# Attention, MoE and a second MLP on one core: scales from sums on ScalarE, the mask inside the minus product, steps laid out anew

## Chip, core and metric

The kernel runs on one core of a Trainium2 chip. The metric is the time of one execution on the device in microseconds. TensorE is called PE here, VectorE DVE, ScalarE ACT, GpSimd POOL and SyncE SP, as in the profile.

## What is computed

Three stages, all in float32 at the interface:

```python
# chunked attention: B=4, H=8, S=768, D=64, chunks of 32, 16 keys left and 8 right, 8 memory keys
scores = scale * q_c @ k_full.T            # k_full = 8 memory keys, then the chunk's window
a = exp(scores - scores.max(-1)); a /= a.sum(-1) + 1e-9
out[:, :, c] = a @ v_full
# MoE: N=3072 tokens, D=512, E=8 experts, F=1024
P = exp(x @ w_gate - max)
for _ in range(8): P /= P.sum(1) + 1e-9; P /= P.sum(0) + 1e-9; P *= N / E
x = sum over e of P[:, e] * (relu(x @ w1[e]) @ w2[e])
# second MLP: 512 to 2048 to 512
out = relu(x @ w_in) ** 2 @ w_out
```

## The kernel before

**Numbers.** Every float32 operand of a matmul is split into a high and a low float16 part, and a product is three float16 matmuls (low by high, high by low, high by high). Before the split an operand is multiplied by a power of two, which a maximum of absolute values sets.

**Attention tiles.** There are 32 tiles of 96 queries. A tile goes through the steps of the table `STEPS`: `load` (five to seven DMAs, issued on SP for the first three tiles and on ACT after that), `mx` (L260: DVE's maximum of absolute values of q, k and v by row, then exponent and cast to `ae`), `row` (L270: PE turns the row values into three rows), `row_mx` (L277, L278: DVE reduces them to three values and puts these on a diagonal `ad`), `all` (L283: PE spreads them to all partitions), `scale` (DVE), `hi` (L326: ACT's high parts), `lo` (L332: DVE's low parts; they free the raw buffer), `tqk` (L338: a transposing DMA on SP), `scores` (L356 adds the mask by a product with a one-hot matrix, L368 the products of q and k), `max` (DVE: maximum over keys, split into `m`), `mt` (L387: PE transposes the maxima), `mtc` (L395: ACT copies them), `st` (L403: the transposed mask; L414: the transposed scores; L417: minus the maxima, by a product with the matrix `minus`), `exp` (L426), `ahi`, `alo` (the split of the exponentials on ACT and POOL), `av` (L447 to L455: the product with v), `norm`, `xhi`, `xlo` (L464 to L481) and `tx` (L491: a transposing DMA into the token tile `xt`). The scores stand in three PSUM buffers, which `scores` and `st` share.

Raw q, k and v of a tile stand in one of three buffers, from tile 18 on in one of two.

**The order.** It is written out by hand. Each step of tile i is put into a list at a planned time, and the list is sorted by it; each engine then runs its own instructions in that order:

```python
def ta(i):
    return T0 + sum(TS[:i]) + TA * max(0, i - len(TS))

def when(i, n):
    r = min(1.0, i / RAMP)
    t = ta(i) + (1 - r) * STEPS[n][1] + r * STEPS[n][0]
    if n == "load" and i >= 3:
        prev = max(m for m in range(i) if raw_of(m) == raw_of(i))
        t = max(t, when(prev, "lo") + LDO)
    return t
```

So from tile 6 on the first offset of a step counts alone, and tiles follow each other by `TA`. Between the steps of the attention tiles stand the units of the first expert: four pairs (`l1_pair`, 24 matmuls of 256 columns) and four halves (`l2_half`, 12 matmuls of 512 columns) for every 256 tokens, each unit 2.65 x `STR` planned units after the one before it, and not before `done(i)`, which is `tx` plus 4, of the last tile they need, plus `DN[1]`. `gate` (eight small matmuls, and a copy by ACT at L515) stands at the start of each block, moved by `DN[2]`.

**After attention.** The gate's weights are balanced in eight rounds on DVE, PE and ACT, beside the end of the first expert. Experts 1 to 7 and the second MLP follow, the later ones with Strassen-like products of seven blocks, whose small steps are put off by the numbers of items in `LAG` and `W1B`. L1133 there makes the low parts of such operands.

**Set-up.** `setup_const` fills the constants, most of them on POOL.

Of the kernel before, what the change touches and what calls it, by code (L numbers as in the profile page):

```python
# [7 lines left out]
F32 = mybir.dt.float32  # L8
# [16 lines left out]
    "all": (2.56, 1.20),  # L25
    "scale": (4.56, 1.59),
    "hi": (7.00, 2.19),
    "lo": (8.20, 2.60),
    "tqk": (15.08, 6.30),
    "scores": (26.35, 11.37),  # L30
    "max": (27.25, 12.18),
    "mt": (30.80, 13.20),
    "mtc": (31.00, 13.30),
    "st": (33.80, 14.20),
    "exp": (34.80, 15.20),
    "ahi": (36.80, 16.20),
    "alo": (37.00, 16.30),
    "av": (42.00, 19.20),
    "norm": (42.60, 19.90),
    "xhi": (45.20, 21.70),  # L40
    "xlo": (47.14, 21.80),
    "tx": (53.00, 23.20),
}
L1LAG = 1.730
T0 = 5.969
TS = [6.83, 3.31, 5.80, 8.23, 10.00]
TA = 10.957
# [4 lines left out]
W_AT = [-5.06, 6.92, 9.11, 14.42, 18.96, 23.87, 33.67, 39.86, -3.33, 28.00, 3.81]  # L52
# [3 lines left out]
DN = [-0.34, 0.00, 0.08]  # L56
# [10 lines left out]
W1B = [[1, 2, 2, 5], [2, 3, 6, 8]]  # L67

LAG = [{"11": [2, 3], "22": [14, 15], "12": [3, 4], "relu": {"c11": 2, "c22": 2, "c12": 1},
# [12 lines left out]
def tile_attention_moe_moe2(  # L82
# [42 lines left out]
    T_QKV = 3  # L125
# [43 lines left out]
    maskr = ap_.tile([TQ, 3, P], BF16, name="maskr")  # L169
    onehot = ap_.tile([TQ, TQ], BF16, name="onehot")  # L170
    ident16 = ap_.tile([TQ, TQ], F16, name="ident16")
    minus = ap_.tile([2 * H, H, P], F16, name="minus")
# [84 lines left out]
    def a_scale(i):  # L257
        raw = raws[raw_of(i)]
        mx = ap_.tile([P, 3], F32, tag="amx", name="amx", bufs=2)
        nc.vector.tensor_reduce(mx, raw, AX.X, ALU.max, apply_absolute_value=True)  # L260
        eb = ap_.tile([P, 3], I32, tag="aeb0", name="aeb0", bufs=2)
        e16 = ap_.tile([P, 3], BF16, tag="ae16", name="ae16", bufs=2)
        nc.vector.tensor_scalar(eb, mx.bitcast(I32), EXP_MASK, None, ALU.bitwise_and)
        nc.vector.tensor_copy(e16, eb.bitcast(F32))
        st[i, "e16"] = e16
# [7 lines left out]
    def a_row_max(i):  # L273
        p = st.pop((i, "rows"))
        g = ap_.tile([3, 1], F32, tag="ag", name="ag", bufs=2)
        d3 = ap_.tile([3, 3], BF16, tag="ad3", name="ad3", bufs=2)
        nc.vector.tensor_reduce(g, p, AX.X, ALU.max)  # L277
        nc.vector.tensor_scalar(d3, ident[0:3, 0:3], g, None, ALU.mult)  # L278
        st[i, "d3"] = d3

    def a_spread(i):
        p = psa.tile([P, 3], F32, tag="mm", name="pall")
        nc.tensor.matmul(p, lhsT=ones16[0:3, :], rhs=st.pop((i, "d3")), start=True, stop=True)  # L283
        st[i, "gm"] = p
# [62 lines left out]
    def mask_of(i):  # L347
        j = i % TPB
        return maskr[:, 0 if j == 0 else (2 if j == TPB - 1 else 1)]

    def a_scores(i):

        qkT = st[i, "qkT"]
        scs = [psa.tile([TQ, 4, P], F32, tag="sc", name="sc", bufs=3) for u in range(2)]
        for sc in scs:
            nc.tensor.matmul(  # L356
                sc,
                lhsT=onehot,
                rhs=mask_of(i).unsqueeze(1).to_broadcast([TQ, 4, P]),
                start=True,  # L360
                stop=False,
            )
# [1057 lines left out]
    def setup_const():  # L1420
        for r in raws:
            nc.gpsimd.memset(r[TQ:P, 0, :], 0.0)
        for t in v16s:
            nc.gpsimd.memset(t[:, 0, :, D:D + 1], 1.0)
        nc.vector.memset(ones, 1.0)
        nc.vector.memset(ones16, 1.0)
        nc.gpsimd.memset(ident, 0.0)
# [3 lines left out]
        nc.gpsimd.memset(onehot, 0.0)  # L1431
        nc.gpsimd.memset(ident16, 0.0)
# [4 lines left out]
        nc.gpsimd.memset(minus, 0.0)  # L1437
        for part in range(2):
            nc.gpsimd.affine_select(
                out=minus, in_=minus, compare_op=ALU.not_equal, fill=-1.0, base=-H * part,  # L1440
                pattern=[[-1, H], [0, P]], channel_multiplier=1)
        nc.gpsimd.memset(maskr, NEG)
        for c in range(TQ // CH):
            rows = slice(c * CH, (c + 1) * CH)
            nc.gpsimd.memset(onehot[rows, rows], 1.0)
            for mv in range(3):
# [5 lines left out]
                nc.gpsimd.memset(maskr[rows, mv, c0:c1], 0.0)  # L1452
                nc.gpsimd.memset(maskr[rows, mv, NW:P], 0.0)
# [369 lines left out]
```

## Time and profile before

| | |
|---|---|
| time, median of 3 runs | 2587.06 us (2585.54 to 2591.34) |
| time of the profiled execution | 2587.19 us |
| its span, first to last instruction | 2585.3 us |
| PE busy | 2445.2 us (95%) |
| DVE busy | 1892.4 us (73%) |
| ACT busy | 1338.0 us (52%) |
| POOL busy | 1337.6 us (52%) |
| mean granted clock of PE | 0.989 |

The span is what the trace covers; the time of the same execution has 1.9 us around it. Busy times leave out the engines' waits and their issuing of DMAs. The attention stage ends near 490 us, the balancing near 590.

### The profile page before, as it was taken

Reading aid. Unit: us, or ns where it says so; the run is one execution under the profiler, and the core shown is the slowest. Engines: PE = TensorE matmul, PEld = TensorE weight load, DVE = VectorE, ACT = ScalarE, POOL = GpSimd, SP = SyncE. Lnnn points to the kernel's source line nnn. Section 1 sums busy time; section 2 is a strip of 40 time slices with the busy share of each in tenths; the row PEclk is TensorE's granted clock in tenths of the full one; section 3 lists DMA queues with packets and bytes.
Section 4 is the critical chain, followed back from the end, with each engine's and each line's share of the span. In section 5 each row is a group of like instructions: output and inputs, shape, how many; then the busy total and the mean of one; then the engine's idle time right before and its main releaser. Section 6 shows DMA issues by size and latency. Waiting matters only on the chain.

```text
span 2585.3 us, 53582 instructions
## 1 busy us (share of the span) xinstructions
PE 2445.2 (95%) x22034; PEld 2043.0 (79%) x22034; DVE 1892.4 (73%) x2896; ACT 1338.0 (52%) x2317; POOL 1337.6 (52%) x1154
## 2 busy tenths in 40 slices
PE   2789899889999999999999999999999989999999
PEld 1566666656677888888888888888888878888887
DVE  6777677386566888788788878877768897666555
ACT  3444344242335555556555555655556666776453
POOL 3311112262554666567467556755746776876443
PEclk9989999989999999999999999999999999999999
DMA  8587766323144435444534533443333365663211
GB/s 166 90 141 133 110 122 100 80 82 103 69 152 172 151 121 175 140 142 123 187 131 139 184 129 130 137 173 128 107 118 123 117 170 158 177 168 123 87 64 47
DMA packets 377917, 334.32 MB, mean 129 GB/s; under 512 B 256584, under 2 KB 311368, under 8 KB 371016
## 3 DMA queue, kind: packets, MB, share of 16 engines
q1 hardware_dynamic: 294054, 309.99, 41.0%
q10 hardware_dynamic: 83618, 20.91, 4.6%
q8 instruction: 172, 2.82, 0.5%
q14 instruction: 73, 0.60, 0.1%
HBM read 215.50 MB, written 77.07 MB: 113 GB/s over the span
## 4 chain that ended last, share of the span: by engine, by line
PE 79%; DVE 10%; issue 3%; ACT 3%; POOL 2%; DMA 2%; SPq 1%; ACTq 1%; DVEq 0%; POOLq 0%
PE pbA L935 34%; PE pbE L935 18%; PE pbB L935 8%; PE pb L935 4%; PE py L1291 3%; PE py L1293 3%; PE py L1292 3%; PE ph L796 1%; PE ph L798 1%; PE ph L797 1%; DVE amx L260 1%; DMA raw<-in_q_dram 1%; PE sc L368 1%; PE sct L414 1%; DVE hp L1133 1%
## 5 line engine op out<-in xcount | busy, mean ns | idle before, releaser
L935 PEld LDWEIGHTS <-wb 128*128 128x128 f16 x5184 | 509.1, 98 | 70.2 <-issue 8.5
L935 PEld LDWEIGHTS <-hp 128*128 128x128 f16 x4608 | 451.0, 98 | 56.4 <-issue 3.9
L935 PEld LDWEIGHTS <-wx 128*128 128x128 f16 x3888 | 381.2, 98 | 51.1 <-issue 6.2
L935 PEld LDWEIGHTS <-xt 128*128 128x128 f16 x3456 | 337.8, 98 | 49.7 <-DVE xt L1133 8.3
L935 PE MATMUL pbA<-w2p,hp 128*128 128x256 f16 x2304 | 290.7, 273 | 2.2 <-ACT S L1063 1.5
L935 PE MATMUL pbE<-xt,wx 128*128 128x256 f16 x2304 | 284.1, 273 | 5.4 <-DVE u L1068 3.7
L935 PE MATMUL pbA<-S,wb 128*128 128x256 f16 x2304 | 283.3, 273 | 4.5 <-ACT S L1063 2.1
L1063 ACT ACTIVATE u<-pbA 128x512 f32<-128x512 f32 x180 | 106.8, 593 | 227.9 <-PE pbA L935 227.5
L438 POOL TENSOR_TENSOR aT<-e,aT 128x768 f16<-128x768 f32 x32 | 52.5, 1641 | 255.3 <-ACT aT L432 223.8
L1063 ACT ACTIVATE xt<-pbA 128x512 f32<-128x512 f32 x147 | 86.7, 593 | 148.1 <-PE pbA L935 146.3
L935 PE MATMUL pbA<-w2p,xt 128*128 128x256 f16 x1152 | 157.1, 273 | 0.0
L935 PE MATMUL pbE<-xt,hp 128*128 128x256 f16 x1140 | 155.9, 273 | 0.0
L935 PE MATMUL pbE<-xt,xt 128*128 128x256 f16 x1140 | 155.5, 273 | 0.2 <-POOL xt L1133 0.2
L1291 PE MATMUL py<-w2p,hp 128*128 128x512 f16 x384 | 148.0, 386 | 4.5 <-DVE hp L926 3.3
L1292 PE MATMUL py<-w2p,hp 128*128 128x512 f16 x384 | 147.2, 383 | 0.0
L1293 PE MATMUL py<-w2p,hp 128*128 128x512 f16 x384 | 147.2, 383 | 0.0
L1068 DVE TENSOR_TENSOR u<-pbE,u 128x512 f32<-128x512 f32 x100 | 68.8, 688 | 105.8 <-ACT u L1063 61.1
L935 PE MATMUL pbB<-xt,wb 128*128 128x256 f16 x1152 | 141.4, 273 | 0.0
L935 PE MATMUL pbA<-xt,wb 128*128 128x256 f16 x1152 | 141.4, 273 | 0.0
L935 PE MATMUL pbA<-S,wx 128*128 128x256 f16 x1152 | 141.4, 273 | 0.0
L1133 POOL TENSOR_TENSOR hp<-u,hp 128x512 f16<-128x512 f32 x86 | 109.1, 1269 | 57.7 <-ACT hp L1126 57.7
L1133 POOL TENSOR_TENSOR xt<-u,xt 128x512 f16<-128x512 f32 x72 | 95.9, 1341 | 55.0 <-ACT xt L1126 55.0
(373 smaller groups left out, 5816.0 us busy)
## 6 DMA issues: line engine op xcount, KB each, us to landing
wst<-in_moe_w_dram SPq DMA_DIRECT2D x80, 512.0 KB
xt<-xdr SPq DMA_DIRECT2D x40, 1024.0 KB
S<-sdr SPq DMA_DIRECT2D x126, 256.0 KB
w2d<-wst SPq DMA_DIRECT2D x32, 512.0 KB
w2p<-w2d SPq DMA_DIRECT2D x32, 512.0 KB
wst<-in_moe_w_dram SPq DMA_DIRECT2D x56, 256.0 KB
xdr<-xt SPq DMA_DIRECT2D x12, 1024.0 KB
w2d<-tw SPq DMA_DIRECT2D x32, 384.0 KB
```

The source lines that it names most:

```text
L260: nc.vector.tensor_reduce(mx, raw, AX.X, ALU.max, apply_absolute_value=True)
L368: nc.tensor.matmul(scs[u][:, hh, :], lhsT=q_, rhs=k_, start=False, stop=(s == 1 and hh == 3))
L414: nc.tensor.matmul(scs[u][:, hh, :], lhsT=k_, rhs=q_, start=False, stop=False)
L438: nc.gpsimd.tensor_tensor(aT[:, 1], st.pop((i, "e")), aT[:, 0], ALU.subtract)
L796: nc.tensor.matmul(p[:, r], lhsT=w[:, 1], rhs=xh, start=first, stop=False)
L935: nc.tensor.matmul(p[:, r], lhsT=w[:, ws], rhs=x[:, xs], start=a, stop=z, skip_group_check=onto)
L1063: nc.scalar.activation(t, p, AF.Copy, scale=sc)
L1068: nc.vector.tensor_tensor(t, p, t, ALU.add)
L1133: eng.tensor_tensor(d[:, 1], t, d[:, 0], ALU.subtract)
L1291: nc.tensor.matmul(p, lhsT=h[:, 1], rhs=w[:, 0], start=first, stop=False)
L1292: nc.tensor.matmul(p, lhsT=h[:, 0], rhs=w[:, 1], start=False, stop=False)
L1293: nc.tensor.matmul(p, lhsT=h[:, 0], rhs=w[:, 0], start=False, stop=last)
```

## The change

`mx` no longer reduces on DVE: ACT takes the absolute values of q, k and v one after the other and writes their sums over each row; exponent and cast stay on DVE, and the constant `T_QKV` of the scale goes from 3 to 9, since a sum of 512 values is larger than their maximum. `st` loses the two mask matmuls of L403: the matrix `minus` becomes `less`, whose first 96 rows hold the mask and whose last 16 the minus ones, and the matmul that transposes the maxima also puts the one-hot rows in front of them, so that one product takes the mask in and the maxima off. The spread (`all`) contracts over all 128 rows of a padded diagonal instead of three. Set-up fills its constants on DVE and builds `less` on ACT. In `STEPS` every offset from `all` to `xlo` falls by 1.61 and that of `tx` rises by 2.39; `TA`, `T0`, `TS`, `DN`, `W_AT`, `LAG` and `W1B` change as shown.

```diff
-    "all": (2.56, 1.20),
-    "scale": (4.56, 1.59),
-    "hi": (7.00, 2.19),
-    "lo": (8.20, 2.60),
...
-    "st": (33.80, 14.20),
-    "exp": (34.80, 15.20),
...
-    "xlo": (47.14, 21.80),
-    "tx": (53.00, 23.20),
+    "all": (0.95, 1.20),
+    "scale": (2.95, 1.59),
+    "hi": (5.39, 2.19),
+    "lo": (6.59, 2.60),
...
+    "st": (32.19, 14.20),
+    "exp": (33.19, 15.20),
...
+    "xlo": (45.53, 21.80),
+    "tx": (55.39, 23.20),
-T0 = 5.969
-TS = [6.83, 3.31, 5.80, 8.23, 10.00]
-TA = 10.957
+T0 = 6.039
+TS = [6.83, 3.56, 5.57, 8.21, 10.00]
+TA = 10.980
-W_AT = [-5.06, 6.92, 9.11, 14.42, 18.96, 23.87, 33.67, 39.86, -3.33, 28.00, 3.81]
+W_AT = [-5.06, 6.92, 9.11, 14.42, 16.84, 23.87, 31.34, 39.86, -3.33, 28.00, 3.81]
-DN = [-0.34, 0.00, 0.08]
+DN = [-1.72, 0.22, -1.33]
-W1B = [[1, 2, 2, 5], [2, 3, 6, 8]]
+W1B = [[1, 2, 2, 5], [3, 3, 5, 8]]
-LAG = [{... "s1": 1, "s2": 2, "r": 2 ...}, {... "12": [3, 4], "relu": {"c11": 1, ...}, "s1": 1 ...}]
+LAG = [{... "s1": 1, "s2": 2, "r": 1 ...}, {... "12": [2, 4], "relu": {"c11": -1, ...}, "s1": -1 ...}]
-    T_QKV = 3
+    T_QKV = 9
-    maskr = ap_.tile([TQ, 3, P], BF16, name="maskr")
+    less = ap_.tile([TQ + 2 * H, 3, H, P], BF16, name="less")
+    maskr = less[0:TQ, :, 0]
-    minus = ap_.tile([2 * H, H, P], F16, name="minus")
+    m16s = [ap_.tile([TQ, TQ + 2 * H], F16, name=f"m16_{n}") for n in range(2)]
+    heads = ap_.tile([TQ + 2 * H, H], BF16, name="heads")
+    ad3s = [ap_.tile([P, 3], BF16, name=f"ad3_{n}") for n in range(2)]
 def a_scale(i):
-        nc.vector.tensor_reduce(mx, raw, AX.X, ALU.max, apply_absolute_value=True)
+        for t in range(3):
+            junk = ap_.tile([P, H * D], BF16, tag="junk", name="junk")
+            nc.scalar.activation(junk, raw[:, t, :], AF.Abs, accum_out=mx[:, t:t + 1])
 def a_spread(i):
-        nc.tensor.matmul(p, lhsT=ones16[0:3, :], rhs=st.pop((i, "d3")), start=True, stop=True)
+        nc.tensor.matmul(p, lhsT=ones16, rhs=st.pop((i, "d3")), start=True, stop=True)
 def a_max(i):
-        m16 = ap_.tile([TQ, 2, H], F16, tag="m16", name="m16", bufs=2)
+        m16 = m16s[i % 2][:, TQ:].rearrange("p (s h) -> p s h", s=2)
 def a_mt(i):
-        p = psa.tile([2 * H, TQ], F32, tag="mm", name="pmt")
-        nc.tensor.matmul(
-            p, lhsT=st.pop((i, "m16")).rearrange("p s h -> p (s h)"), rhs=ident16,
-            start=True, stop=True)
+        p = psa.tile([TQ + 2 * H, TQ], F32, tag="mm", name="pmt")
+        nc.tensor.matmul(p, lhsT=m16s[i % 2], rhs=ident16, start=True, stop=True)
 def a_st(i):
-        for sc in scs:
-            nc.tensor.matmul(
-                sc,
-                lhsT=mask_of(i),
-                rhs=onehot.unsqueeze(1).to_broadcast([TQ, 4, TQ]),
-                start=True,
-                stop=False,
-            )
...
-                    nc.tensor.matmul(scs[u][:, hh, :], lhsT=k_, rhs=q_, start=False, stop=False)
+                    nc.tensor.matmul(scs[u][:, hh, :], lhsT=k_, rhs=q_, start=(s == 0 and hh == 0), stop=False)
...
-                    scs[u][:, hh, :], lhsT=minus[:, 4 * u + hh], rhs=mt,
+                    scs[u][:, hh, :], lhsT=less[:, mask_at(i), 4 * u + hh], rhs=mt,
 def setup_const():
+        fill = nc.vector.memset
...
+        for mv in range(3):
+            nc.scalar.activation(
+                less[TQ:, mv], heads[TQ:].unsqueeze(2).to_broadcast([2 * H, H, P]), AF.Copy)
+            nc.scalar.activation(
+                less[0:TQ, mv, 1:], maskr[:, mv].unsqueeze(1).to_broadcast([TQ, H - 1, P]), AF.Copy)
```

## Rows read from the trace of the kernel before

**Rows 1.** Busy time by stretch: engine busy us (instructions), granted clock, DMA share, GB/s.

```profile
60.00:150.00 90.00, 66.01 (x689) 49.32 (x689) 64.95 (x146) 40.70 (x76) 26.60 (x28) 0.89 0.62 101
150.00:440.00 290.00, 268.44 (x2776) 188.56 (x2774) 216.88 (x517) 127.20 (x255) 54.11 (x79) 0.99 0.73 122
...
490.00:640.00 150.00, 129.77 (x818) 83.18 (x816) 99.05 (x172) 47.30 (x70) 63.19 (x54) 0.93 0.31 105
640.00:1960.00 1320.00, 1318.06 (x11699) 1143.60 (x11697) 1009.90 (x1337) 707.52 (x1183) 772.85 (x623) 1.00 0.42 139
1960.00:2260.00 300.00, 282.89 (x2544) 249.82 (x2542) 240.55 (x356) 198.57 (x347) 220.46 (x171) 0.99 0.54 152
```

The engines stand in the order PE, PEld (PE's weight loads), DVE, ACT, POOL.

**Rows 2.** Waits of PE, 0 to 60 us: total us, times, longest.

```profile
PE pmax L270 <- DVE ae L264: 24.9, 2, 17.4
PE pmt L387 <- DVE m L381: 8.1, 1, 8.1
```

**Rows 3.** Waits of PE, 60 to 150 us.

```profile
PE pmt L387 <- DVE agm L288: 9.4, 3, 4.6
PE pmax L270 <- DVE ae L264: 5.5, 2, 3.1
```

**Rows 4.** Waits of PE, 150 to 490 us.

```profile
PE pmax L270 <- DVE ae L264: 6.7, 5, 3.7
PE sc L356 <- ACT e L426: 5.5, 7, 1.2
...
PE pall L283 <- DVE ad L278: 3.5, 3, 2.5
```

**Rows 5.** Chain that ended last, 260 to 330 us: start, us, what.

```profile
302.28 9.00 DMA raw<-in_q_dram
```

**Rows 6.** Timeline of PE, 200 to 212 us: start, us, instruction.

```profile
200.57 0.23 PE L447 MATMUL av<-v,aT 128*96 128x65 f16 x1
...
201.63 0.21 PE L455 MATMUL av<-v,aT 128*96 128x65 f16 x1
...
205.33 0.49 PE L403 MATMUL sct<-onehot,maskr 96*128 96x384 bf16 x2
...
205.65 0.78 PE L414 MATMUL sct<-qkT 128*128 128x96 f16 x16
...
206.37 0.51 PE L417 MATMUL sct<-mt,minus 16*128 16x96 f16 x8
...
207.43 0.39 PE L1291 MATMUL py<-w2p,hp 128*128 128x512 f16 x1
...
210.03 0.60 PE L356 MATMUL sc<-maskr,onehot 96*96 96x512 bf16 x2
```

**Rows 7.** Groups by line, 150 to 440 us: busy us, mean ns, idle before.

```profile
L260 DVE TENSOR_REDUCE amx<-acc 128x3 f32<-128x1536 f32 x12 | 20.9, 1745 | 1.4 <-DMA acc<-in_q_dram 1.2
L260 DVE TENSOR_REDUCE amx<-raw 128x3 f32<-128x1536 f32 x9 | 15.7, 1749 | 5.7 <-DMA raw<-in_q_dram 5.4
...
L326 ACT ACTIVATE v<-acc,asc 128x512 f16<-128x512 f32 x12 | 8.5, 709 | 0.0
...
L515 ACT ACTIVATE lg<-lgp 128x16 f32<-128x16 f32 x16 | 2.9, 182 | 5.3 <-PE lgp L508 5.3
```

**Rows 8.** Timeline of ACT, 299 to 333 us; ACTq is its issuing of DMAs.

```profile
300.44 0.33 ACTq L235 DMA_DIRECT2D raw<-in_k_dram  x1
...
302.28 0.55 ACTq L252 DMA_DIRECT2D raw<-in_q_dram  x1
302.93 0.63 ACT L476 ACTIVATE x<-acc 96x512 f16<-96x512 f32 x1 [2.36 <-DMA raw<-in_mem_v_dram]
```

**Rows 9.** Timeline, 26.6 to 27.8 us: row matmul and spread.

```profile
26.71 0.27 PE L270 MATMUL pmax<-ident,ae 128*3 128x128 bf16 x1 [7.49 <-DVE ae L264]
...
27.60 0.16 PE L283 MATMUL pall<-ad,ones 3*128 3x3 bf16 x1 [0.62 <-DVE wm L640]
```

**Rows 10.** Waits of PE, 1960 to 2260 us.

```profile
PE pbB L935 <- DVE xt L1133: 6.4, 3, 2.3
```

More of the change, by code (lines that the diff above doesn't have):

```diff
@@ L24 @@
     "row_mx": (0.16, 0.90),
-    "all": (2.56, 1.20),
-    "scale": (4.56, 1.59),
-    "hi": (7.00, 2.19),
-    "lo": (8.20, 2.60),
[L29 to L33, printed above, removed]
-    "st": (33.80, 14.20),
-    "exp": (34.80, 15.20),
[L36 to L40, printed above, removed]
-    "xlo": (47.14, 21.80),
-    "tx": (53.00, 23.20),
+    "all": (0.95, 1.20),
+    "scale": (2.95, 1.59),
+    "hi": (5.39, 2.19),
+    "lo": (6.59, 2.60),
+    "tqk": (13.47, 6.30),
+    "scores": (24.74, 11.37),
+    "max": (25.64, 12.18),
+    "mt": (29.19, 13.20),
+    "mtc": (29.39, 13.30),
+    "st": (32.19, 14.20),
+    "exp": (33.19, 15.20),
+    "ahi": (35.19, 16.20),
+    "alo": (35.39, 16.30),
+    "av": (40.39, 19.20),
+    "norm": (40.99, 19.90),
+    "xhi": (43.59, 21.70),
+    "xlo": (45.53, 21.80),
+    "tx": (55.39, 23.20),
 }
 L1LAG = 1.730
-T0 = 5.969
-TS = [6.83, 3.31, 5.80, 8.23, 10.00]
-TA = 10.957
+T0 = 6.039
+TS = [6.83, 3.56, 5.57, 8.21, 10.00]
+TA = 10.980
 STR = 1.413
@@ L275, in a_row_max @@
         g = ap_.tile([3, 1], F32, tag="ag", name="ag", bufs=2)
-        d3 = ap_.tile([3, 3], BF16, tag="ad3", name="ad3", bufs=2)
+        d3 = ad3s[i % 2]
         nc.vector.tensor_reduce(g, p, AX.X, ALU.max)
-        nc.vector.tensor_scalar(d3, ident[0:3, 0:3], g, None, ALU.mult)
+        nc.vector.tensor_scalar(d3[0:3], ident[0:3, 0:3], g, None, ALU.mult)
         st[i, "d3"] = d3
@@ L345, in qk_of, with mask_at @@
         return ((qkT[:, h, 0:TQ], qkT[:, n, :]), (qkT[half, H + h // 2, 0:TQ], qkT[half, n, :]))
-    def mask_of(i):
+    def mask_at(i):
         j = i % TPB
-        return maskr[:, 0 if j == 0 else (2 if j == TPB - 1 else 1)]
+        return 0 if j == 0 else (2 if j == TPB - 1 else 1)
     def a_scores(i):
@@ L358, in a_scores @@
                 lhsT=onehot,
-                rhs=mask_of(i).unsqueeze(1).to_broadcast([TQ, 4, P]),
+                rhs=maskr[:, mask_at(i)].unsqueeze(1).to_broadcast([TQ, 4, P]),
                 start=True,
@@ L381, in a_max @@
         nc.vector.tensor_tensor(m16[:, 1], m, m16[:, 0], ALU.subtract)
-        st[i, "m16"] = m16
     def a_mt(i):
-        p = psa.tile([2 * H, TQ], F32, tag="mm", name="pmt")
-        nc.tensor.matmul(
-            p, lhsT=st.pop((i, "m16")).rearrange("p s h -> p (s h)"), rhs=ident16,
-            start=True, stop=True)
+        p = psa.tile([TQ + 2 * H, TQ], F32, tag="mm", name="pmt")
+        nc.tensor.matmul(p, lhsT=m16s[i % 2], rhs=ident16, start=True, stop=True)
         st[i, "pmt"] = p
@@ L393, in a_mtc @@
         p = st.pop((i, "pmt"))
-        mt = ap_.tile([2 * H, TQ], F16, tag="mt", name="mt", bufs=2)
+        mt = ap_.tile([TQ + 2 * H, TQ], F16, tag="mt", name="mt", bufs=2)
         nc.scalar.activation(mt, p, AF.Copy)
@@ L1420, in setup_const @@
     def setup_const():
[L1421 to L1427, printed above, removed]
+        fill = nc.vector.memset
+        fill(ident, 0.0)
         nc.gpsimd.affine_select(
@@ L1430, in setup_const @@
             pattern=[[-1, P]], channel_multiplier=1)
-        nc.gpsimd.memset(onehot, 0.0)
-        nc.gpsimd.memset(ident16, 0.0)
+        fill(ident16, 0.0)
         nc.gpsimd.affine_select(
@@ L1435, in setup_const @@
             pattern=[[-1, TQ]], channel_multiplier=1)
-        nc.gpsimd.memset(minus, 0.0)
+        fill(heads, 0.0)
         for part in range(2):
             nc.gpsimd.affine_select(
-                out=minus, in_=minus, compare_op=ALU.not_equal, fill=-1.0, base=-H * part,
-                pattern=[[-1, H], [0, P]], channel_multiplier=1)
-        nc.gpsimd.memset(maskr, NEG)
+                out=heads[TQ:], in_=heads[TQ:], compare_op=ALU.not_equal, fill=-1.0,
+                base=-H * part, pattern=[[-1, H]], channel_multiplier=1)
+        fill(ones, 1.0)
+        fill(ones16, 1.0)
+        for t in ad3s:
+            fill(t, 0.0)
+        for r in raws:
+            fill(r[TQ:P, 0, :], 0.0)
+        for t in v16s:
+            fill(t[:, 0, :, D:D + 1], 1.0)
+        fill(maskr, NEG)
+        fill(onehot, 0.0)
+        for t in m16s:
+            fill(t, 0.0)
         for c in range(TQ // CH):
             rows = slice(c * CH, (c + 1) * CH)
-            nc.gpsimd.memset(onehot[rows, rows], 1.0)
+            for t in (onehot, *m16s):
+                fill(t[rows, rows], 1.0)
             for mv in range(3):
@@ L1451, in setup_const @@
                     c1 -= RIGHT
-                nc.gpsimd.memset(maskr[rows, mv, c0:c1], 0.0)
-                nc.gpsimd.memset(maskr[rows, mv, NW:P], 0.0)
+                fill(maskr[rows, mv, c0:c1], 0.0)
+        fill(maskr[:, :, NW:P], 0.0)
+        for mv in range(3):
[3 more added lines that the diff above has]
+                less[0:TQ, mv, 1:], maskr[:, mv].unsqueeze(1).to_broadcast([TQ, H - 1, P]), AF.Copy)
     with tc.manual_schedule():
```

6 rows, old and new, of the table LAG are left out of this document.

## Prediction

> **What bounds the kernel now.** I read the table by stretches first, for PE's busy time in each [rows 1]. From 640 to 1960 us PE is busy 1318.06 of 1320 us: nothing to win there. The idle time lies before and beside that: 24.0 us from 60 to 150, 21.6 in the steady part of the attention stage from 150 to 440, 20.2 in the passage from 490 to 640 and 17.1 from 1960 to 2260. The change touches the attention stage by its instructions and the rest by its numbers.
>
> Then the waits of PE, stretch by stretch. In the first 60 us PE waits for DVE: 24.9 us at L270, which needs the exponents of the row maxima, and once 8.1 us at L387 for the score maxima [rows 2]. From 60 to 150 it is DVE again, 9.4 and 5.5 us [rows 3]. From 150 to 490 the list is mixed: 6.7 us for DVE's `ae`, 5.5 for ACT's exp, 3.5 for DVE's `ad` [rows 4]. Part of the DVE waits are a late load in disguise: the chain, which names what PE's work hung on last, runs through a load of q for 9.00 us, one of three such loads between 260 and 330 us [rows 5]. So PE's own work bounds the stage, with DVE's order and some late loads on top.
>
> **The change part by part.**
>
> *The mask matmuls.* L403 goes: two matmuls a tile. They start at 205.33 and the next line starts at 205.65 [rows 6], so 0.32 us a tile, 32 tiles: 10.2 us. The minus product (L417) and the transposition of the maxima (L387) get 112 rows instead of 16, but the same number of streamed columns; I cost that at nothing. Bounds: not below zero, since no instruction goes by it; above, 1 us a tile, if each of their nine weight loads stood bare. They stand among matmuls whose loads run ahead, so I take 0.
>
> *The scales.* DVE loses a reduction of 1.745 us a tile; ACT gains three Abs of 128x512. An ACT pass over such a source takes 0.709 us in L326 [rows 7]. The trace has no Abs and no summed output, so I bound one from below by the 0.63 us of L476 [rows 8] and from above by L326 plus a small extra instruction like the gate's copy, 0.182 us [rows 7]: 1.9 to 2.7 us a tile. I take 2.1, nearest to L326. The 21 reductions of the steady part [rows 7] put tiles 13.8 us apart; ACT is busy 127.2 of its 290 us [rows 1], and a load's issues hold it 2.4 us, from 300.44 to 302.83 [rows 8]. That makes 44% + 17% + 15%, 76%: it fits, with little air.
>
> A rule speaks against this part. An fp32 column costs DVE 1.745/1536 us, 1.14 ns, and ACT 0.709/512, 1.38 ns [rows 7]: about the same. The Trainium skill, "ScalarE: Activation LUTs", section "Rules for kernel authors", would keep relu, max and add on VectorE, which it puts at up to about three times faster per element in bf16; the trace does not agree for fp32 sources.
>
> *Where Abs stands.* A step's place is its tile's start plus an offset; tiles start 10.957 (new 10.980) planner units apart. Abs (-3.44, or 29.50 of the tile three earlier) comes on ACT right behind that tile's copy of maxima (29.39). After `mt` PE has the product with v (200.57 to 201.63), in most tiles one expert unit (2.6 us, as the twelve matmuls from 207.43 to 210.03), and the transposed scores without masks (205.65 to 206.88) [rows 6]: 1.1 + 2.6 + 1.2 = 4.9 us up to L270. The chain copy, Abs, exponent, cast is 0.3 + 2.1 + about 0.5 with its hand-overs, 2.9 us. So Abs is hidden with 2 us to spare. In five tiles no unit stands there, and PE waits some 0.6 us; those are tiles in which PE now waits for exp (5.5 us in all [rows 4]), which it then finds done. Net 0. Behind Abs on ACT queue an expert relu, the next load's issues, the split of x and exp. Exp comes some 1.2 us later behind the scores than now; the next scores need its first half 3.7 us after them, so that too is hidden.
>
> *The spread.* All offsets from "all" on fall by 1.61, but "row" stays at -0.44. Before, `st` of the tile three earlier stood at 33.80 - 32.87 = 0.93, between row (-0.44) and all (2.56). Now it stands at 32.19 - 32.94 = -0.75, ahead of both, and all at 0.95. Expert units come every 2.65 x 1.413 = 3.74 units, so a gap of 1.39 holds one in about a third of the tiles. Laying out all places by the constants I count, in tiles 8 to 31, 17 with nothing on PE between L270 and L283, where before only tile 8 was so and most had 4 us of work. PE then sits through DVE's two small steps. With DVE free they took 27.60 - 26.71 = 0.89 us from start to start [rows 9], of which 0.15 is L270 itself: 0.74 x 17 = 12.6 us, 13 with two tiles that have only gates there. Bounds: 10, if tiles slip against each other, to 25, if DVE is busy with a split each time.
>
> *What goes in return.* DVE's split of the tile before now precedes the exponent step, and DVE has 1.75 us less a tile. The waits for `agm`, `ae` and `ad` after 60 us sum to 9.4 + 5.5 + 6.7 + 3.5 = 25.1 us [rows 3, 4]. The loads profit too: from tile 18 on two buffers alternate, and a load stands 2.806 behind the split that frees its buffer; that split moves up by 1.61, so the load gets 8.95 units ahead of its use instead of 7.47, at some 1.25 us a unit enough for 9.00 us [rows 5]. Bounds 5 to 25; I take 15. In the first 60 us, `max` of tile 1 now stands ahead of tile 4's exponent step instead of behind its reduction and a split; of the 8.1 us [rows 2] I take 3 (0 to 6). The very first chain gets 0.4 us longer (2.1 for 1.745), inside that bound.
>
> *Set-up.* 37 fills move to DVE and six ACT copies are added, some 5 and 7 us. Both engines are free until the first q has landed, as PE's wait at L270 shows [rows 2]: 0. Without that cover, the two would run into the first chain and cost up to 3 us.
>
> *Passage and second half.* The expert blocks move 2.6 to 2.9 units later and the tile steps 0.9 earlier, so more of PE's work stands behind the last tile; its total is the same. The 20.2 us of idle time in the passage [rows 1] hang on other work: 0, bounds -3 to +3. LAG and W1B shift some small steps; from 640 to 1960 that can win nothing. From 1960 to 2260 PE waits 6.4 us for a low half in L1133 [rows 10]; the high half before it now comes one step sooner: -2, bounds -7 to +4. The granted clock is 0.89 from 60 to 150 [rows 1], some 20 us at 1.2 GHz, in the stretch with the most waits; with fewer of them I take -2, bounds -5 to +3.
>
> Sum: -10.2 + 13 - 15 - 3 - 2 - 2 = -19.2 us. The profiled execution has a span of 2585.3 and a time of 2587.19, so 1.9 lies around the span; it stands 0.1 above the median of 2587.06. 2585.3 - 19.2 + 1.9 = **2568.0 us**.
>
> **The rivals.**
>
> *The waits only change places.* PE gets 10.2 us less work, the new stop at the spread eats 13, and of the 25.1 us of waits only 5 go, because the loads are late for another reason: they share DMA engines that are busy 0.73 of the steady part [rows 1]. 2587.2 - 10.2 + 13 - 5 = 2585. For it: the stop follows from the order alone. Against: the late loads are the largest single waits, and they do get more lead.
>
> *ACT becomes the bound: slower.* The place is the exponent step behind Abs. It decides once three Abs take over 4.1 us a tile, the 2.1 plus the 2 us to spare. If each took 1.6 us, a second pass for the sum, that is 4.8 us: PE stands 0.7 us at each of 23 steady tiles, and exp slips a further 2.7 us, of which half a microsecond shows at the scores. 1.2 x 23 = 28 us on top of the forecast: 2596. For it: 76% is much for an engine that works in order and issues loads between. Against: much of ACT's idle time is waiting for PE, and no row of the trace shows a second pass.
>
> *ACT three times as slow as DVE.* 3 x 1.745 = 5.2 us, 1.1 us over the point: 1.1 + 0.5 a tile, 37 us, 2605. That is the rule weighed above, the Trainium skill's "ScalarE: Activation LUTs"; the fp32 rows speak against it, 2 in 100.
>
> *More goes.* All 25 us of waits after 60 us, 6 before, 7 in the second half: 2587.2 - 10.2 + 13 - 25 - 6 - 7 - 2 = 2550.
>
> **How the numbers follow.** Chances: forecast 0.58 (its own range 2556 to 2580), places changed 0.20, ACT the bound 0.10, three times as slow 0.02, more goes 0.10. About 0.2%, 5.2 us, is what a measurement of this kernel tells from no change: 2581.9 to 2592.2. The forecast gives 0.56 faster and 0.02 same; places changed splits into 0.06, 0.09 and 0.05; with the other three, faster 0.72, same 0.11, slower 0.17. For eight in ten I reach from 2551, which leaves out half of "more goes", to 2592, which leaves out most of the two ACT cases.
>
> **What would show it.** Right: no L403 and no 1.745 us reduction; three Abs of 0.6 to 0.9 us a tile on ACT; at the spread a wait of about 0.7 us for `ad` in some 17 tiles; waits for `ae` after 150 us under 3 us; tiles less than 13.4 us apart in the steady part. Wrong: Abs over 1.2 us; PE waiting for `ae` in most tiles; ACT held by a load at Abs; new waits between 640 and 1960; more of the stage at half clock than now.

## The result, and the profile after

The changed kernel takes 2615.03 us (median of 4 runs, 2612.58 to 2618.75); the kernel before, run beside it on the same chip, 2589.2 (4 runs, 2585.54 to 2591.72). The ratio is 1.0099, interval 1.0087 to 1.0111: it is slower by 1%. The forecast was 2568.0 with a range up to 2592, so the prediction was wrong, in its sign too.

By stretch, columns as in [rows 1], the changed kernel gives:

```profile
60.00:150.00 90.00, 56.89 (x630) 43.72 (x631) 49.49 (x143) 47.05 (x100) 24.44 (x24) 0.82 0.64 103
150.00:440.00 290.00, 249.06 (x2498) 176.52 (x2498) 171.60 (x457) 156.66 (x354) 55.85 (x75) 0.92 0.71 114
490.00:640.00 150.00, 132.51 (x971) 89.92 (x969) 94.96 (x170) 50.73 (x79) 56.60 (x48) 0.94 0.25 82
640.00:1960.00 1320.00, 1317.71 (x11604) 1134.15 (x11603) 1018.49 (x1328) 694.38 (x1166) 776.18 (x616) 1.00 0.42 140
1960.00:2260.00 300.00, 282.81 (x2535) 249.51 (x2533) 241.72 (x368) 196.13 (x344) 217.06 (x167) 0.98 0.51 143
```

From 640 us on PE is as little idle as before: 2.3 and 17.2 us in the last two stretches, 1.9 and 17.1 before. The loss stands in the attention stage: PE's idle time there was 24.0 + 21.6 us in the first two stretches [rows 1] and is now 33.1 + 40.9, 28.4 more. ACT's busy time in the steady part rose from 127.2 to 156.7, DVE's fell from 216.9 to 171.6. The transposition of the maxima of tile 5 starts at 125.6 us (125.9 before), that of tile 31 at 498.1 (470.9 before): from tile 5 on tiles follow each other by 14.3 us instead of 13.3, and by tile 31 the kernel is 27.2 us late, of the 29.4 by which the two profiled spans differ.

The waits of PE (total us, times, longest), first from 0 to 60 us, then 60 to 150, then 150 to 490, to be held against [rows 2], [rows 3] and [rows 4]:

```profile
PE pmax L279 <- DVE ae L273: 32.5, 4, 17.6
PE pall L292 <- DVE ad L287: 9.7, 3, 7.2
...
PE pmax L279 <- DVE ae L273: 6.9, 3, 3.2
PE pmt L395 <- DVE m L390: 5.6, 1, 5.6
...
PE pall L292 <- DVE ad L287: 16.0, 15, 2.4
PE sc L365 <- ACT e L424: 14.6, 9, 5.2
PE ph L794 <- ACT lg L513: 8.1, 6, 2.7
PE pmax L279 <- DVE rs L462: 6.2, 7, 2.1
```

The wait for the exponents of the row maxima, 6.7 us in the steady part before, is gone from the list (the 6.2 us booked on L462, which DVE runs right behind the cast, may be the same delay), and none of the loads of q that stood in the chain between 260 and 330 us [rows 5] stands there now. But the spread (L292) waits in 15 tiles, exp (L424) makes PE wait 14.6 us for 5.5 before, and there is a wait that the kernel before did not have. It is on DVE, 60 to 490 us, the head of the list:

```profile
DVE aeb L272 <- ACT junk L269: 38.6, 25, 6.1
```

DVE's exponent step (L272) stands still for ACT's Abs (L269) in 25 tiles. Abs itself, with durations in ns (least, median, most):

```profile
L269 ACT ACTIVATE junk<-acc x57: 613/629/633, 27.0 to 465.8; 128x512 bf16<-128x512 f32 x57
L269 ACT ACTIVATION_READ_ACCUMULATOR junk<-acc x57: 185/186/205, 27.6 to 466.3; 128x1 f32 x57
```

One tile of the steady part shows how the waits come about. ACT, then DVE, then PE between 257 and 265 us (start us, us, instruction, idle time before it):

```profile
257.31 0.24 ACT L401 ACTIVATE mt<-pmt 112x96 f16<-112x96 f32 x1
257.44 0.63 ACT L269 ACTIVATE junk<-acc 128x512 bf16<-128x512 f32 x1
...
259.48 0.19 ACT L269 ACTIVATION_READ_ACCUMULATOR junk<-acc 128x1 f32 x1
259.99 0.78 ACTq L241 DMA_DIRECT2D raw<-in_v_dram  x1
...
262.30 0.57 ACTq L258 DMA_DIRECT2D raw<-in_q_dram  x1
262.97 0.63 ACT L474 ACTIVATE x<-acc 96x512 f16<-96x512 f32 x1 [3.30 <-DVE ad L287]
263.51 1.03 ACT L424 ACTIVATE e<-sct,sce 128x384 f32<-128x384 f32 x2
```

```profile
259.70 0.17 DVE L272 TENSOR_SCALAR aeb<-amx 128x3 int32<-128x3 int32 x1 [1.63 <-ACT junk L269]
...
260.40 0.69 DVE L465 TENSOR_TENSOR acc<-av,rs 96x512 f32<-96x512 f32 x1
261.01 0.68 DVE L803 SCALAR_TENSOR_TENSOR hp<-ph,hp 128x512 f16<-128x512 f32 x1
261.61 0.67 DVE L607 TENSOR_REDUCE wmx<-acc 128x1 f32<-128x512 f32 x1
262.20 0.27 DVE L286 TENSOR_REDUCE ag<-pmax 3x1 f32<-3x128 f32 x1
```

```profile
258.44 0.51 PE L415 MATMUL sct<-mt,less 112*128 112x96 f16 x8
...
261.47 0.22 PE L279 MATMUL pmax<-ident,ae 128*3 128x128 bf16 x1
262.78 0.16 PE L292 MATMUL pall<-ad,ones 128*128 128x3 bf16 x1 [1.09 <-DVE ad L287]
...
264.12 0.59 PE L365 MATMUL sc<-less,onehot 96*96 96x512 bf16 x1 [0.92 <-ACT e L424]
...
266.08 0.61 PE L1289 MATMUL py<-w2p,hp 128*128 128x512 f16 x1
...
267.28 0.38 PE L1289 MATMUL py<-w2p,hp 128*128 128x512 f16 x1
```

Abs follows the copy of the maxima on ACT. Behind it come the issues of a load (to 262.87), the split of x, and only at 263.51 the exp, though its transposed scores (L415) were done by 258.95; the 3.30 us of idle time booked on `ad` ahead of the split are these issues, which do not count as busy. DVE stands 1.63 us, and then does the rest of its queue late: the reduction that PE needs for the spread (L286) comes at 262.20, 0.5 us after its input was there, behind two pieces of expert work. PE stops twice in this tile, at the spread and at the next scores, and the expert matmul behind the stops (266.08) takes 0.61 us instead of the 0.38 of the same one at 267.28: the granted clock is 0.50 from 264.0 to 267.2, which is 1.2 GHz, and 1.00, 2.4 GHz, from 267.2 to 270.

### The profile page after: what moved, and what is told of

It reads as the page before. It is cut to its first block, busy times and chain, and to the rows that moved or that the text cites. A ratio compares the mean times of both kernels' runs of the same rounds, so it can differ in the third digit from the quotient of the medians.

```text
span 2614.7 us, 53748 instructions
## 1 busy us (share of the span) xinstructions
PE 2439.7 (93%) x21970; PEld 2043.0 (78%) x21970; DVE 1852.5 (71%) x2900; ACT 1403.7 (54%) x2515; POOL 1346.7 (52%) x1120
## 4 chain that ended last, share of the span: by engine, by line
PE 77%; DVE 9%; ACT 5%; issue 3%; DMA 2%; ACTq 2%; POOL 1%; SPq 1%; DVEq 0%; POOLq 0%
PE pbA L933 34%; PE pbE L933 17%; PE pbB L933 8%; PE pb L933 4%; PE py L1289 3%; PE py L1290 3%; PE py L1291 3%; PE ph L794 1%; PE ph L795 1%; PE ph L796 1%; ACT junk L269 1%; DVE hp L1131 1%; DVE acc L1244 1%; ACTq L255 1%; PE sc L377 1%
## 5 line engine op out<-in xcount | busy, mean ns | idle before, releaser
L1131 POOL TENSOR_TENSOR hp<-u,hp 128x512 f16<-128x512 f32 x86 | 115.4, 1342 | 64.7 <-ACT hp L1124 64.7
L794 PE MATMUL ph<-xt,wb 128*128 128x256 f16 (+1 forms) x416 | 116.0, 284 | 11.8 <-ACT lg L513 8.1
```

What stands on the lines that cost most here:

```text
L794: nc.tensor.matmul(p[:, r], lhsT=w[:, 1], rhs=xh, start=first, stop=False)
L1131: eng.tensor_tensor(d[:, 1], t, d[:, 0], ALU.subtract)
```

## The experiments

Each was timed beside the kernel before, which took 2587.1 to 2588.6 us on those chips. DVE reduction means the old line with `T_QKV = 3`.

**The parts apart.** Four kernels take mask and order, or Abs and order, singly.

```diff
 # mask_old: the changed kernel with all planned numbers of before and
-        for t in range(3):
-            junk = ap_.tile([P, H * D], BF16, tag="junk", name="junk")
-            nc.scalar.activation(junk, raw[:, t, :], AF.Abs, accum_out=mx[:, t:t + 1])
+        nc.vector.tensor_reduce(mx, raw, AX.X, ALU.max, apply_absolute_value=True)
 # mask_new: the same edit, with the numbers of the change
 # both_old: the changed kernel (Abs kept) with all planned numbers of before
 # abs_old: the kernel before with Abs for the reduction and T_QKV = 9, nothing else
```

> The changed kernel with all planned times, LAG and W1B of before, and with the reduction for the scales back on DVE (T_QKV 3). What is left of the change is the mask in the minus product and the new set-up. Order theory (the new places of the steps cost the time) and ACT theory (Abs on ACT costs it) both expect the mask's 10 us: 2575 to 2580 us, half-clock time in the attention stage as before. If the larger minus product or transposition cost something after all: 2587 or more.

> The changed kernel with its new order, but with the reduction for the scales back on DVE (T_QKV 3). Order theory: slow, 2600 to 2615 us, with waits of 0.7 us or more at the spread in 15 tiles and the clock at half for 40 us of the stage. ACT theory: fast, 2570 to 2580, since the waits for exp and for the gate's copy go.

> The changed kernel, Abs on ACT included, with all planned times, LAG and W1B of before. Order theory: close to the mask alone, 2572 to 2585 us, with few waits at the spread and a granted clock near 0.99 from 150 to 440 us. ACT theory: slow, 2605 to 2620, with waits for exp (L365) above 10 us.

> The kernel before with one edit: absolute sums by three Abs on ACT instead of the reduction on DVE (T_QKV 9). Order theory: 2580 to 2592 us, no loss. ACT theory: 2605 to 2620 us, with waits for exp above 10 us.

| kernel | median us (range, runs) | ratio to before |
|---|---|---|
| mask_old | 2576.33 (2573.43 to 2578.38, 4) | 0.9954 [0.9939, 0.9969] |
| mask_new | 2588.86 (2587.29 to 2591.28, 10) | 1.0 [0.9988, 1.0012] |
| both_old | 2623.58 (2619.31 to 2627.71, 4) | 1.0134 [1.0115, 1.0154] |
| abs_old | 2634.95 (2632.18 to 2637.51, 4) | 1.0181 [1.0166, 1.0196] |

The joined mask is worth 2576.3 - 2587.9 = -11.6 us; the new set-up and the spread over 128 rows are in that number too and were not run apart. In mask_old's trace tiles 5 to 31 follow each other by 12.9 us, 0.4 less than before. The new order alone costs 2588.9 - 2576.3 = +12.5. Abs costs 47 us in the old order, with the mask joined (2623.6 against 2576.3) or not (2635.0 against 2587.9), and 26 in the new (2615.0 against 2588.9). So it is Abs that turns the sign, and the new order takes 21 of its 47 us back while it costs 12.5 itself. Neither theory on record had the size: mask_new lies between the two, both_old and abs_old lie above both. And in the old order it is not the waits for exp that grow, as the texts on record expected (above 10 us; 6.7 in both_old and 5.7 in abs_old, from 150 to 490 us), but those for `ae`: 24.2 and 19.0 us, where mask_old has 8.9 and the kernel before 6.7 [rows 4].

The waits of PE from 150 to 490 us, mask_old:

```profile
PE pmax L277 <- DVE ae L271: 8.9, 6, 3.9
...
PE pall L290 <- DVE ad L285: 4.1, 4, 2.0
```

and mask_new:

```profile
PE pall L290 <- DVE ad L285: 17.4, 15, 2.4
```

The order alone, without Abs, makes the stop at the spread: waits in 4 tiles become waits in 15.

In abs_old, PE 150 to 490 us, then DVE 60 to 490 us:

```profile
PE pmax L272 <- DVE ae L266: 19.0, 10, 3.9
...
DVE aeb L265 <- ACT junk L262: 91.3, 26, 6.0
```

**DVE's wait for Abs.** Two kernels make exponent and cast a step `ex` of their own, behind what DVE can do meanwhile; abs_old_late is that on abs_old, after_late on the changed kernel.

```diff
+    "ex": (-0.6, 0.5),
     "row": (-0.44, 0.60),
```

> Abs on ACT in the old order as in abs_old, but with exponent and cast as a step of its own on DVE, put off from -3.44 to -0.60, right ahead of the row matmul. Queue theory: the 75 us of DVE's waits for Abs shrink below 30, the time falls from 2635 to 2595 to 2612 us. Occupancy theory: no change, 2628 to 2640, or slower, since PE then waits for the exponent.

> The changed kernel with exponent and cast put off in the same way, to -0.60. Queue theory: the 58 us of DVE's waits for Abs fall by half, 2595 to 2608 us. Occupancy theory: 2612 to 2620, as before the edit.

abs_old_late took 2648.19 us (2647.48 to 2652.41, 4 runs; ratio 1.0231 [1.02, 1.0263]), after_late 2605.36 (2601.89 to 2608.99, 6 runs; 1.0065 [1.0043, 1.0087]). DVE hardly waits for Abs any more, 2.6 and 5.6 us from 60 to 490. In the old order PE pays for it:

```profile
PE pmax L277 <- DVE ae L271: 33.9, 18, 3.4
```

33.9 us in place of 19.0, and 13 us slower, where the queue theory on record expected 23 to 40 us less. In the new order PE waits only 8.2 us in 8 tiles for `ae`, and 9.7 us are gained. So in these two orders delaying the step helped only where it did not make PE wait for the exponents instead.

**Numbers of the order, singly.**

```diff
 # mask_new_steps_old: mask_new with the table STEPS of before
 # mask_old_units: mask_old with W_AT and DN of the change
 # mask_old_pace: mask_old with T0, TS and TA of the change
```

> The mask in the minus product, reduction on DVE, LAG, W1B and DN of the change, but STEPS, T0, TS and TA of before: it undoes the shift of 1.61 by which the row matmul and the spread came to stand next to each other. Order theory (the stop at the spread is what the new order costs): 2573 to 2580 us, waits at the spread below 6 us after 150 us. Otherwise (the other numbers cost it): 2585 to 2592.

In this kernel only `STEPS` went back; `T0`, `TS` and `TA` were those of the change, other than the text on record says. Read it so.

> The kernel with the mask joined to the product with the maxima, the row maxima on DVE and all planned times of before (2576.3 us), but with W_AT and DN of the change: the weights' preparation 2.1 and 2.3 units earlier, gates 1.4 earlier, units 0.2 later. With T0, TS, TA, LAG and W1B of the change too it took 2585.0 us. Theory 'the units' places cost it': most of the 8.7 us return, 2582 to 2588 us. Rival 'it is the tiles' pace (T0, TS, TA)': 2574 to 2579 us.

> The kernel with the mask joined, the row maxima on DVE and all planned times of before (2576.3 us), with T0, TS and TA of the change alone. W_AT and DN of the change cost 1.4 us (2577.8); all numbers but STEPS cost 8.7. Theory 'the tiles' pace': 2582 to 2588 us. Rival 'LAG and W1B, or the numbers together': 2574 to 2579 us.

mask_new_steps_old took 2585.03 us (10 runs, 0.9982 [0.9968, 0.9997]), mask_old_units 2577.75 (6 runs, 0.9954 [0.994, 0.9968]), mask_old_pace 2587.33 (11 runs, 1.0002 [0.9993, 1.0011]). Against mask_old's 2576.3 that is +8.7, +1.4 and +11.0. The pace of the tiles, `T0`, `TS` and `TA` together, costs by itself nearly all of the order's 12.5 us; the parts do not simply add, since all numbers but `STEPS` cost less than the pace alone. `LAG` and `W1B` were not run alone. The shift of `STEPS` costs 3.8 on top of the other new numbers, at the edge of what a measurement tells, though it brings 13 us of waits to the spread (4.4 us in 8 tiles with the old table, 17.4 in 15 with the new); other waits fall at the same time, that for exp from 7.3 to 2.6. In mask_old_pace PE's waits are a little longer in many places and in none by over 5 us; which of the three numbers does it, and by which unit, stays open.

**Abs that nobody reads.** In the kernel before, reduction kept, three Abs a tile write sums into a tile that no one reads: ACT's time alone. Then they are moved.

```diff
 # dead_abs, ahead of the reduction in the step at -3.44
+        dead = ap_.tile([P, 3], F32, tag="dead", name="dead", bufs=2)
+        for t in range(3):
+            junk = ap_.tile([P, H * D], BF16, tag="junk", name="junk")
+            nc.scalar.activation(junk, raw[:, t, :], AF.Abs, accum_out=dead[:, t:t + 1])
 # the same four lines as a step of their own: dead_abs_mtc, dead_abs_hi, dead_abs_free
+    "ab": (-1.80, -0.50),
+    "ab": (7.10, 2.30),
+    "ab": (4.80, 1.80),
```

> The kernel before with three Abs on ACT at the place of the change whose sums nobody reads; DVE's reduction stays. It adds work and changes no value. Queue theory (the cost is that DVE's exponent step stands in DVE's queue waiting for Abs and holds up what is behind it): 2588 to 2602 us. Occupancy theory (2.3 us a tile are too much for ACT, whoever reads them): 2618 to 2640 us, as with the sums in use.

> The kernel before, with three more Abs a tile on ACT whose sums nobody reads, as a step of its own planned right behind ACT's copy of the maxima (offset -1.80; the copy of the tile three earlier falls at -1.87) instead of at -3.44, ahead of it. With the dead Abs ahead of the copy the time was 2613.4 us and PE waited 17.7 us in 13 tiles for the transposed maxima. Theory 'place in ACT's queue': the 17.7 us go, and with them most of the loss; something comes back at exp and relu, which now stand close behind; 2592 to 2602 us. Rival 'ACT's time': 2.3 us a tile on ACT cost the same wherever they stand, because ACT or the memory is short; 2608 to 2620 us.

> The kernel before, with three more Abs a tile on ACT whose sums nobody reads, right behind ACT's high parts of the same tile (offset 7.10), where nothing that PE needs within the next 10 units waits for ACT but the relu of an expert unit and gate copies. The raw buffer is held a little longer. Theory 'place in ACT's queue': within 8 us of before, 2587 to 2596 us, and no group of PE's waits grows by over 6 us. Rival 'ACT's time': 2608 to 2620 us as with the dead Abs elsewhere.

> The kernel before, with three more Abs a tile on ACT whose sums nobody reads, at offset 4.80: in ACT's cycle of 10.957 units that is behind the split of the exponentials (36.80, which is 3.93) and ahead of the high parts (7.00). The dead Abs at 7.10 stood at nearly the same place in the cycle as at -3.44 (which is 7.52): both directly ahead of the copy of the maxima (31.00, which is 9.09), so the pair could not tell place from time. Theory 'place in ACT's queue': 2.2 units of slack ahead of the high parts take most of it, 2590 to 2600 us, and PE's wait for the copied maxima falls under 8 us from 150 us on. Rival 'ACT's time': 2606 to 2618 us wherever they stand, with that wait still above 12 us.

| kernel | median us (range, runs) | ratio to before |
|---|---|---|
| dead_abs | 2613.4 (2612.04 to 2615.24, 4) | 1.0092 [1.0055, 1.0128] |
| dead_abs_mtc | 2607.4 (2601.44 to 2608.14, 4) | 1.0071 [1.0055, 1.0087] |
| dead_abs_hi | 2613.73 (2611.22 to 2620.05, 4) | 1.0098 [1.0081, 1.0115] |
| dead_abs_free | 2599.73 (2596.96 to 2599.93, 4) | 1.0045 [1.0031, 1.0058] |

dead_abs lies between the two theories on record, so the queue on DVE is not all of the price. The premise of dead_abs_hi was a slip of mine: ACT's order repeats every 10.957 units, so 7.10 is the place of -3.44 (7.52) over again, behind the high parts and ahead of the copy of the maxima (9.09); it is a repeat of dead_abs and gives its time. Ahead of the copy, PE waits for that copy in the old order, 150 to 490 us, dead_abs:

```profile
PE pmax L274 <- ACT mt L399: 17.7, 13, 3.6
```

L274 needs the PSUM buffer that the copy reads. In the free stretch, dead_abs_free, it is down to:

```profile
PE pmax L278 <- ACT mt L403: 4.0, 5, 1.0
```

The place halves the price, from 26 to 12.7 us. The other 12.7 stay even there, so the rival may have a part of the truth; they are at most what ACT's time costs by itself, since no run shows that this place delays nothing. Sums that are read would have to stand there one tile's spacing earlier, at -6.16, since `row` needs them before; whether the load has landed by then was not tried. Behind the copy (dead_abs_mtc) the wait for it goes too (1.4 us), but 8.9 us for exp stand there instead of 5.8, and only 6 us come back, which leaves the time just below the rival's range.

**What DVE's relief is worth.** The reduction over 64 of 512 columns takes 0.34 us instead of 1.745, so DVE is relieved of 1.4 us a tile, and ACT gets nothing: in mask_old (short_old) and in mask_new (short_new). Then the Abs are put beside it unread, at their place in the change (short_new_dead), and in a free place (short_new_free).

```diff
-        nc.vector.tensor_reduce(mx, raw, AX.X, ALU.max, apply_absolute_value=True)
+        nc.vector.tensor_reduce(mx, raw[:, :, 0:64], AX.X, ALU.max, apply_absolute_value=True)
 # short_new_free, with the four lines above as a step of their own
+    "ab": (3.20, 1.80),
```

> The kernel with the mask joined, the row maxima on DVE and all planned times of before (2576.3 us), but with the maxima taken over the first 64 of 512 values of q, k and v; ACT gets nothing. It shows what freeing DVE of the long reduction is worth by itself, apart from Abs. Theory 'freeing DVE helps and Abs takes more than that': 2562 to 2572 us, the waits for ae from 150 us on under 4 us. Rival 'DVE's reduction was hidden': 2573 to 2579 us.

> The changed kernel with the row maxima on DVE again, over the first 64 of 512 values, and nothing of it on ACT: the new order with the relief of DVE that the change was to bring, and without the cost on ACT. With the full reduction on DVE it took 2588.9 us, the changed kernel 2615. Theory 'freeing DVE helps': 2570 to 2583 us, so that the new order only pays with a scale that costs neither engine. Rival 'the stop at the spread is what holds it': 2584 to 2590 us, with about 15 us of waits for ad left.

> The new order with the maxima over 64 of 512 values on DVE (2572.0 us), and beside it the three Abs of the change on ACT, at their place in the change, with sums that nobody reads. Against the changed kernel (2615.0 us) only the wait of DVE's exponent step for Abs is gone, and a short reduction is added. Theory 'half occupancy of ACT, half DVE's wait': 2592 to 2602 us. Rival 'all is ACT's occupancy': 2608 to 2616 us. Rival 'all is DVE's wait': 2570 to 2578 us.

> As short_new_dead, with the unread Abs at offset 3.20 of the new order: in ACT's cycle of 10.98 units behind the split of the exponentials (2.25) and ahead of the high parts (5.39), not ahead of the copy of the maxima (29.39, which is 7.43). In the old order that place halved the price of unread Abs, from 26 to 12.7 us. If place sets the price in the new order too: 2580 to 2588 us, and below short_new_dead. Rival 'in the new order the place ahead of the copy costs nothing more': within 4 us of short_new_dead.

| kernel | median us (range, runs) | ratio to before |
|---|---|---|
| short_old | 2558.34 (2556.03 to 2560.0, 4) | 0.9887 [0.9873, 0.99] |
| short_new | 2571.95 (2567.68 to 2574.14, 4) | 0.9934 [0.9919, 0.995] |
| short_new_dead | 2601.7 (2598.16 to 2602.39, 5) | 1.0043 [1.0027, 1.0059] |
| short_new_free | 2581.7 (2577.32 to 2584.58, 10) | 0.9975 [0.9962, 0.9989] |

DVE's relief is worth 18.0 us in the old order, more than the text on record expected, and 16.9 in the new. Unread Abs cost 29.7 us at their place and 9.7 in the free one. The text on record for short_new_free names the wrong neighbour: in the new order Abs stands just behind the copy of the maxima (7.54 against 7.43 in the cycle), and ahead of the load's issues and of exp. That is what the waits show, PE from 150 to 490 us, in short_new, short_new_dead and short_new_free in turn:

```profile
PE sc L363 <- ACT e L422: 4.9, 6, 1.5
PE ph L792 <- ACT lg L511: 4.3, 3, 2.3
```

```profile
PE sc L367 <- ACT e L426: 13.9, 8, 3.3
PE ph L796 <- ACT lg L515: 8.2, 5, 2.6
```

```profile
PE ph L800 <- ACT lg L519: 9.5, 5, 3.9
...
PE sc L371 <- ACT e L430: 2.8, 4, 0.9
```

With Abs at its place PE waits 13.9 us for exp, in the free place 2.8. By the starts in tiles 8 to 31 of the traces, exp begins a median of 0.33 us after the first half of the transposed scores in the kernel before, 2.50 in mask_new, 1.87 in short_new, 3.30 in short_new_dead, 2.22 in short_new_free and 2.87 in the changed kernel. So most of the delay against the kernel before comes with the new order, without any Abs; unread Abs at its place add 1.4.

**The account.** From before to after, each step one difference of medians: joined mask -11.6, new order +12.5, DVE relieved -16.9, Abs on ACT +29.7 (at most 9.7 for the time, the other 20.0 for the place), DVE's wait for the sums +13.3 (2615.0 - 2601.7; the short reduction goes in the same step, so the wait is worth a little more and the relief as well). The steps form one chain, so that their sum, +27.0, is 2615.0 - 2587.9 by construction and proves nothing; against the kernel before of the same runs the difference is 2615.0 - 2589.2 = +25.8. In another order the parts have other sizes, as the 47 us for Abs in the old order show.

## Why the prediction was wrong

**Right.** The mask matmuls: -10.2 forecast, -11.6 measured, the new set-up included. The two products with 112 rows cost about the zero I took: in mask_old PE is busy 17.9 us with the one and 7.2 with the other over all tiles, 17.8 and 6.9 before. What one tile's Abs takes: 1.9 to 2.7 us forecast, and 2.23 in the tile shown, from 257.44 to the end of the last read-out at 259.67. The stop at the spread: 17 tiles and 13 us forecast, 15 tiles and 10.1 (after_late) to 17.4 us (mask_new) of waits in the kernels with the new order. The tiles were counted well, one stop was priced too low: of the 0.89 us in [rows 9] I gave L270 0.15 and took 0.74 as idle, the rows have 0.27 and 0.62, and in the changed kernel a stop takes 16.0/15 = 1.07 us. The sum's -15 for DVE's relief has the size of the 16.9 and 18.0 measured when nothing went to ACT. That the loads of q would leave the chain came true in the changed kernel, but in short_new, which has the new order and the relief, a load of q stands in it for 7.00 us at 308.05, so the longer lead is not shown to be the reason.

**The step that failed is "Abs is hidden with 2 us to spare ... Net 0", with its tail "that too is hidden".** I followed the one path from Abs to PE's row step (L279), and that one held: in the tile shown, the exponents are there at 260.07 and PE comes for them at 261.47. The working named only ACT's work as queued behind Abs, and took its delay as covered. Neither end of that holds.

- On ACT, behind Abs stand a load's issues and then exp. The 1.2 us by which exp was to slip are near the 1.4 that unread Abs add; what was wrong is "that too is hidden". The new order had already put exp 2.50 us behind the scores (mask_new), and in the tile shown PE comes to the second of the next scores at 263.20, while exp's first half starts at 263.51 and PE waits 0.92 us. PE waits 14.6 us for exp in the stage, instead of 5.5 before and 2.6 in mask_new. Unread Abs at this place cost 29.7 us against 9.7 in a free place.
- On DVE, the exponent step reads a sum from ACT, which is a new wait at the head of an in-order queue: 38.6 us in 25 tiles. Normalization, the low parts of expert and x, and the row reduction for the spread stand behind it. The text did not name it. Between sums that are read and sums that are not lie 13.3 us.

The net term of 0 for Abs is thus +43.0 us (29.7 + 13.3), against the 16.9 that DVE's relief is worth. The rival "ACT becomes the bound" named the right engine and the wrong condition: it wanted over 4.1 us a tile, and 2.23 did it, for the most part through the order and not through a full engine (ACT is busy 54% of the steady part). For the same reason "ACT three times as slow" is not what happened: an Abs pass with its read-out costs 0.75 us per 512 columns, DVE's reduction 1.745/3 = 0.58 [rows 7]. The Trainium skill's "ScalarE: Activation LUTs", "Rules for kernel authors", lists `max` and `add` among the work for VectorE, and here the kernel that leaves the scale on VectorE is the faster one (mask_new, 2588.9 us, against 2615.0). The ratio of the two times is 1.3 for these fp32 rows; no run here has them in bf16.

**A second step was missing: the pace.** The sum gave `T0`, `TS` and `TA` no term and no reason for that. Alone they cost 11.0 us, most of what the order costs. The spread's +13 was near the count of waits but is not a price: the table's shift costs 3.8 us, with other waits falling. That +13 stands so near the order's measured 12.5 is luck.

**Smaller terms.** In the first 60 us the 8.1 us for the score maxima went, and waits for `ae` and `ad` grew from 24.9 and 6.1 us to 32.5 and 9.7; tile 5 stands at 125.6 us where it stood at 125.9, so the -3 did not come. `LAG` and `W1B`: -2 forecast; from 1960 to 2260 PE's idle time is 17.2 us (17.1 before), so nothing of it shows, and against 6.4 us [rows 10] stands:

```profile
PE pbB L933 <- DVE xt L1131: 6.1, 3, 2.1
```

The clock: -2 forecast, and the granted clock fell, from 0.89 to 0.82 and from 0.99 to 0.92 in the first two stretches; what that is worth stands in the last section. Of the five signs that I listed for a wrong forecast one came clearly, more of the stage at half clock; ACT was held by a load at Abs in only two tiles after 60 us, for 1.9 us in all. The sign for a right one, "tiles less than 13.4 us apart", failed with 14.3, but it was a poor test: 290 us over 21 reductions gave me 13.8 us for the kernel before, whose tiles are 13.3 apart by their starts.

mask_old, the joined mask with the old order and the reduction on DVE, beats both kernels at 2576.3 us and computes the same. short_old's 2558.3 is no such version, since it leaves seven eighths of the values out of the maxima, but it shows that some 18 us lie in a scale that takes 1.4 us a tile from DVE and burdens ACT with nothing.

## What to carry to other kernels

Moving work to an engine with idle time is costed by its place in two in-order queues, and not by its length alone: list what stands behind it on the engine that takes it, and what stands behind the instruction on the old engine that now has to wait for the result. Put an unread copy of the moved work at its place, and a cheap stand-in for it on the old engine: two kernels then give the price and the worth apart. And give each changed number of a hand-laid order a term in the sum, the pace of the tiles first.

## What the hardware showed beyond that

A sum over a row with Abs is two instructions on ACT: 629 ns for 128x512 from fp32 and a read-out of 186 ns that overlaps it in part (257.44 to 258.07 and 257.95 to 258.15 in the tile shown); the three of a tile start 0.75 us apart.

In a single stretch, lower granted clock and time did not go together. From 60 to 150 us, columns as in [rows 1], dead_abs:

```profile
60.00:150.00 90.00, 60.20 (x620) 44.20 (x620) 56.84 (x129) 45.98 (x97) 24.04 (x24) 0.89 0.52 83
```

and dead_abs_hi:

```profile
60.00:150.00 90.00, 62.47 (x650) 47.30 (x649) 58.72 (x136) 48.28 (x101) 24.01 (x24) 0.71 0.56 91
```

0.89 and 0.71, and the two kernels take 2613.4 and 2613.7 us. mask_old has 0.76 there and is 11.6 us faster than the kernel before with its 0.89. Over the whole span it shows. mask_new and then the changed kernel, columns as in [rows 1]:

```profile
0.00:2586.90 2586.90, 2425.73 (x21970) 2035.59 (x21970) 1912.32 (x2932) 1338.99 (x2323) 1346.99 (x1120) 0.98 0.46 129
0.00:2614.70 2614.70, 2439.65 (x21970) 2042.98 (x21970) 1852.46 (x2900) 1403.72 (x2515) 1346.73 (x1120) 0.98 0.46 128
```

PE does the same 21970 matmuls in both. Of the 27.8 us between the spans 13.9 are longer busy time and 13.9 more idle time (161.2 and 175.0 us). The mean granted clock is 0.983 and 0.979; as an estimate from these two, the time at half clock is 88 and 110 us, and the 22 us more would cost 11 if PE were busy throughout. So about half of what Abs costs in the new order, net of the relief, shows as matmuls that take longer, and PE's idle time alone does not rank the kernels: from 60 to 490 us it is 49.8 us in short_old, 53.5 in short_new, 74.5 in short_new_dead and 80.3 in the changed kernel (430 less PE's busy time there), in the order of their times, but 74.6 in abs_old, which takes 20 us longer than the changed kernel.
